# Sums in the fold on VectorE, a narrowing cut in four, and half a sum between two multiply-adds

## The chip, the core and the metric

The kernel runs on one core of a Trainium2 chip. The metric is the device time of one execution in microseconds (us), the median of several runs. Five engines work side by side, each through its own queue in order: TensorE (matmuls, PE in the profile; PEld are its weight loads), VectorE (DVE), ScalarE (ACT), GpSimd (POOL) and SyncE (SP, which here issues DMAs). They wait for each other through semaphores.

## The reference

```python
# x: (8, 3136, 256); w_in: (256, 1024); conv_w: (3, 1024); w_out: (1024, 256), all float32
X = np.fft.fft(x, axis=1)
X = np.fft.fft(X, axis=2)
x = X.real

h = np.maximum(x @ w_in, 0.0)
hp = h with one row of zeros in front of and behind each sequence
conv_out = sum(conv_w[k] * hp[:, k:k + 3136, :] for k in range(3))
gate = 1.0 / (1.0 + np.exp(-conv_out))
out = (h * gate) @ w_out
```

A two-dimensional Fourier transform whose real part is kept, then a feed-forward block whose gate is a convolution of three taps along the sequence.

## The kernel before

**The transform.** The Fourier transform along the sequence is a product with cosine and sine tables. Symmetry is used first: rows of x are added to and subtracted from each other (the "fold"), so that a quarter of the sequence is left to multiply. The rows of a batch come in two halves, each a tile `xh` of up to 99 partitions and eight row blocks of 512 values: four by a plain DMA of SyncE, four in reverse order by indirect DMAs of POOL (L132). `fold_ops(b)` returns seven pieces for each half: `pair(0)` and `pair(2)` (L157) add the mirrored blocks; `both(6, subtract)` (L168) writes the differences of blocks 0, 1 and 2, 3 into blocks 6, 7; `feats(1)` (L189, L190, and small copies on POOL, L191) folds these along the features into a tile `w`; then the sums of blocks 0, 1 and 2, 3; `evens` (L173, L174) adds and subtracts the two sums; `feats(0)` folds that.

The sums have two forms. For batch 0 they are one VectorE instruction, `both(4, add)`. For the other seven batches they are `sums` (L177), an accumulating DMA issued by POOL that adds blocks 2, 3 into blocks 0, 1 of the same tile; `evens` then reads blocks 0, 1 and writes 4, 5.

Nine "units" of matmuls for batch 0 and eight for each later one multiply `w` by the tables (tile `pd`); ScalarE copies one part out of PSUM (L290, L309) and VectorE finishes (`u.fin`: L294, L297, L313, L315, L325, L327) into the tiles `pt` and `qt`.

**The steps.** The feature transform is merged into `w_in`, giving the weights `G`. What remains runs in 256 steps (b, c, f): 8 batches, 4 chunks of the sequence, 8 blocks of 128 features. A step has `seed` (ScalarE, L657, a start value into the PSUM tile `pa`), `products` (TensorE, `pa` and `pb`), `copies` (ScalarE, L689, `pb` scaled into `nb`), `combine` (VectorE, L700, two instructions: `pa` plus `nb` gives the front half of `h`, `pa` minus `nb` the back half, both cut at zero), `first_tap` (ScalarE, L706), `tap` 1 and 2 (VectorE, L711, one multiply-add each), `sigmoid` (ScalarE, L724, in two parts), `gate` (VectorE L732 and POOL L731, one part each; L734 for a rest) and `mm2` (TensorE, `po`, the product with `w_out`; after the eighth feature block ScalarE copies to `os`, L751, and SyncE stores). In steps 3 to 19 (`triple`) TensorE does a third product and ScalarE writes the front half of `h` (L686), and `combine` has one instruction.

**The order.** Everything is recorded by one loop over cycles t, and each engine runs its share in the order of recording. Cycle t holds `sigmoid` of step t-2; `products` and `copies` of step t+1; `combine` of step t, `seed` of step t+2 and `first_tap` of step t; `tap` 1 of step t-1; side work "dve"; `tap` 2 of step t-1; `gate` of step t-2; side work "load"; `mm2` of step t-3; side work "pe". `at(cycle, where, fn)` lists the side work: fold pieces and finishes are under "dve", loads and, before the change, `sums` under "load". `ends` = [9, 20, 36, 61, 93, ...] spreads each batch's fold and units over the steps of the batches before it: batch 1 is folded in cycles 9 to 19, batch 2 in 20 to 35, batch 3 in 36 to 60. `free` keeps the fold pieces of batches 2 and up out of cycles that have a finish or a piece already. Tiles rotate: `pa` has two buffers, `nb` two, `h` four, `g` five, `os` three, `xh` two.

**The narrowing.** The weights come as 64-bit numbers, and VectorE makes 32-bit ones of them: exponent (`power`: L528, then ScalarE L530), mask of the fraction (L542), the low word added to it (L543), the sign (L536), the product (L546). `w_in[3]` and four parts of `w_out` are narrowed within the steps, in cycles 0, 2, 3, 5 and 7: `power` at the cycle's start ("first"), the four others between the two taps ("dve").

Of the kernel before, what the change touches and what calls it, by code (L numbers as in the profile page):

```python
# [11 lines left out]
U32 = mybir.dt.uint32  # L12
AF = mybir.ActivationFunctionType
ALU = mybir.AluOpType
# [19 lines left out]
BIG = 3.4028234663852886e38  # L34
# [3 lines left out]
def kernel(  # L38
# [10 lines left out]
    nc = tc.nc  # L49
# [12 lines left out]
    NF = F // P  # L62
# [24 lines left out]
    vt = nc.vector.tensor_tensor  # L87
    gt = nc.gpsimd.tensor_tensor
    stt = nc.vector.scalar_tensor_tensor
# [12 lines left out]
    xh, wt, ea = {}, {}, {}  # L102
# [39 lines left out]
    def fold_ops(b):  # L142

        def half(h):
            k = slice(0, NP if h == 0 else KR)
            qs = slice(2 * h, 2 * h + 2)

            def t():
                return xh[b, h]

            def pair(m):
                def f():
                    a, r = t()[k, m:m + 2], t()[k, 7 - m:5 - m:-1, ::-1, :]
                    vt(a[:, :, :, 1:D], a[:, :, :, 1:D], r[:, :, :, D - 1:0:-1], op=ALU.add)  # L157
                    if m == 2:
                        a, r = t()[k, 0:4], t()[k, 7:3:-1, ::-1, :]
                        vt(a[:, :, :, 0], a[:, :, :, 0], r[:, :, :, 0], op=ALU.add)  # L160
                return f

            def flat(i, j):
                return t()[k, i:j].rearrange("p s q d -> p (s q d)")

            def both(to, op):
                def f():
                    vt(flat(to, to + 2), flat(0, 2), flat(2, 4), op=op)  # L168
                return f

            def evens():
                f, to = (0, 4) if b else (4, 0)
                vt(flat(to, to + 1), flat(f, f + 1), flat(f + 1, f + 2), op=ALU.add)  # L173
                vt(flat(to + 1, to + 2), flat(f, f + 1), flat(f + 1, f + 2), op=ALU.subtract)  # L174

            def sums():
                nc.gpsimd.dma_start(out=flat(0, 2), in_=flat(2, 4), accum_op=ALU.add)  # L177

            def feats(odd):
                def f():  # L180
                    if h == 0 and odd:
                        wt[b] = [wp.tile([P, 4, HQ, P], F32, name="w", tag="w%d" % i) for i in range(2)]
                        if b == 0:
                            ea[b] = ep.tile([P, 2, HQ], F32, name="ea", tag="ea")
                            nc.gpsimd.memset(wt[b][0][0:KR, 2:4, :, P - 1:P], 0.0)
                    w, s = wt[b][odd], 6 if odd else 4 if b else 0
                    v = t()[k, s:s + 2]
                    lo, hi = v[:, :, :, 1:P], v[:, :, :, D - 1:P:-1]
                    vt(w[k, 0:2, qs, 1:P], lo, hi, op=ALU.add)  # L189
                    vt(w[k, 2:4, qs, 0:P - 1], lo, hi, op=ALU.subtract)  # L190
                    nc.gpsimd.tensor_copy(w[k, 0:2, qs, 0], v[:, :, :, 0])  # L191
                    if b:
                        nc.gpsimd.memset(wt[b][odd][k, 2:4, qs, P - 1:P], 0.0)
                    elif odd:
                        gt(w[k, 2:4, qs, P - 1], t()[k, 7:5:-1, :, P], sg[k], op=ALU.mult)
                    else:
                        nc.gpsimd.tensor_copy(ea[b][k, :, qs], v[:, :, :, P])
                return f

            return [pair(0), pair(2), both(6, ALU.subtract), feats(1), sums if b else both(4, ALU.add),  # L200
                    evens, feats(0)]

        return half(0) + half(1)


# [62 lines left out]
    def product(o, w, st, q, cols, start, stop):  # L268

        def f(p):  # L270
            k = KR if q == HQ - 1 else NP
            mm(p[o], w(k, q), table(k, st, q, cols), start, stop)
        return f
# [240 lines left out]
    def narrow(dst, raw, room=None):  # L514


        ts = nc.vector.tensor_scalar
        lsl, lsr = ALU.logical_shift_left, ALU.logical_shift_right
        lo, hi = raw[:, :, :, 0], raw[:, :, :, 1]
        lof, d = lo.bitcast(F32), dst.bitcast(I32)  # L520
        sg = hi
        if room is not None:
            c, n = hi.shape[1:]
            sg = room[:, 0:c * n].rearrange("p (c n) -> p c n", c=c)

        def power():

            ts(out=d, in0=hi, scalar1=20, scalar2=0x7FF, op0=lsr, op1=ALU.bitwise_and)  # L528
            if room is not None:
                act(d, d, AF.Relu, scale=2.0 ** 23, bias=low[0:d.shape[0]])  # L530
            else:
                ts(out=d, in0=d, scalar1=-896, scalar2=0, op0=ALU.add, op1=ALU.max)
                ts(out=d, in0=d, scalar1=23, scalar2=None, op0=lsl)

        def sign():
            stt(out=d, in0=hi, scalar=-0x80000000, in1=d, op0=ALU.bitwise_and, op1=ALU.bitwise_or)  # L536

        def product():

            if room is None:  # L540
                sign()
            ts(out=sg, in0=hi, scalar1=0xFFFFF, scalar2=0x100000, op0=ALU.bitwise_and, op1=ALU.bitwise_or)  # L542
            stt(out=lof, in0=lo.bitcast(U32), scalar=2.0 ** -32, in1=sg, op0=ALU.mult, op1=ALU.add)  # L543
            if room is not None:
                sign()
            stt(out=dst, in0=lof, scalar=2.0 ** -20, in1=dst, op0=ALU.mult, op1=ALU.mult)  # L546
        return power, product

    class Weight:

# [108 lines left out]
    def triple(s):  # L659

        return s[0] == 0 and TRIPLE[0] <= s[1] * NF + s[2] < TRIPLE[1]
# [26 lines left out]
            for i, cols in enumerate((ch.fcols, ch.cols)):  # L688
                act(nb[s][:, i, cols], p[:, cols], AF.Copy, scale=-1.0 if i else 1.0)  # L689

    def combine(s):

        ch, n, fs = cut(s)
        a, c = pa.pop(s), nb.pop(s)
        if not triple(s):
            row_of(s)
        h = hs[s]
        for i, (to, cols) in enumerate(((h[:, ch.front], ch.fcols), (h[:, ch.back][:, ::-1], ch.cols))):
            if i or not triple(s):
                nc.vector._custom_dve(TENSOR_ADD_SAT, out=to, in0=a[:, cols], in1=c[:, i, cols],  # L700
                                      s0=BIG, s1=0.0)

    def first_tap(s):
        n = chunks[s[1]].w - 2
# [3 lines left out]
    def tap(s, k):  # L708
        g, h, f = gs[s], hs[s], s[2]
        n = g.shape[1]  # L710
        stt(out=g, in0=h[:, k:k + n], scalar=cw[:, k, f:f + 1], in1=g, op0=ALU.mult, op1=ALU.add)  # L711
# [14 lines left out]
    def gate(s):  # L726

        b, c, f = s
        g, h = gs[s], hs.pop(s)[:, 1:]
        v, p, r = shares(s)  # L730
        gt(g[:, p], g[:, p], h[:, p], op=ALU.mult)  # L731
        vt(g[:, v], g[:, v], h[:, v], op=ALU.mult)  # L732
        if r.start < r.stop:
            gt(left[:, f, b % 2 * LEFT:(b % 2 + 1) * LEFT], g[:, r], h[:, r], op=ALU.mult)  # L734
# [81 lines left out]
    side = {}  # L816

    def at(cycle, where, fn):
        side.setdefault((cycle, where), []).append(fn)
# [4 lines left out]
    room = left[:, NF // 2:].rearrange("p f i -> p (f i)").bitcast(I32)  # L824

    def shared(cycle, w, c):
        for where, fn in zip(("first", "dve"), w.parts(c, c + 2, room)):
            at(cycle, where, fn)

    shared(0, w_in[3], 0)  # L830
# [43 lines left out]
        at(cs[-1] - 2, "load", lambda b=b: spread(b, range(len(chunks) - 1)))  # L874
        at(per * b + 1, "load", lambda b=b: spread(b, [len(chunks) - 1]))
    for b in range(1, B):

        ops = fold_ops(b)
        sums = [ops.pop(11), ops.pop(4)]
        m = len(ops) // 2  # L880
        c0, n = ends[b - 1], ends[b] - ends[b - 1]
        cs = [free(c0 + j * n // len(ops)) if b > 1 else c0 + j * n // len(ops) for j in range(len(ops))]
        assert cs[-1] < ends[b] and (b > 1 or cs[m] > NF + 3)
        if b + 1 < B:
            for h in range(2):
                for j, fn in enumerate(load_ops(b + 1, h, nc.sync)):
                    at(cs[m * h + m - 1] + 1 + j, "load", fn)
        for j, fn in enumerate(ops):
            at(cs[j], "dve", fn)
            if j % m == 2:  # L890
                at(cs[j], "load", sums.pop())

# [7 lines left out]
    for t in range(n + LAG):  # L902
        def run(where):
            for fn in side.get((t, where), []):
                fn()
        if 0 <= t - 2 < n:
            sigmoid(steps[t - 2])
        run("first")
        if t + 1 < n:
            products(steps[t + 1])  # L910
            copies(steps[t + 1])
        run("act")
        if t < n:
            combine(steps[t])
        if t + 2 < n:
            seed(steps[t + 2])
        if t < n:
            first_tap(steps[t])

        if 0 <= t - 1 < n:  # L920
            tap(steps[t - 1], 1)
        run("dve")
        if 0 <= t - 1 < n:
            tap(steps[t - 1], 2)
        if 0 <= t - 2 < n:
            gate(steps[t - 2])
        run("load")
        if t >= LAG:
            mm2(steps[t - LAG])
        run("pe")  # L930
# [66 lines left out]
```

## Time and profile before

| what | value |
|---|---|
| median of 3 runs | 1204.5 us (1204.35, 1204.5, 1206.42) |
| the profiled execution's own time | 1206.42 us |
| its span, first to last instruction | 1204.7 us |
| granted TensorE clock, mean | 0.999 |
| TensorE busy | 1170.8 us, 97% |
| VectorE busy | 1111.8 us, 92% |
| ScalarE busy | 883.8 us, 73% |
| GpSimd busy | 480.7 us, 40% |
| accumulating DMAs in the fold (L177) | 14, of 392 or 396 KB each, 5.3 and 5.6 us to landing |
| VectorE taps (L711) | 512, mean 1128 ns |
| VectorE half sums (L700) | 495, mean 557 ns |

In the profile's lines "DVE L173 xh<-xh" is VectorE's instruction of line 173 that writes and reads a tile `xh`. An "idle before" or a bracket with an arrow names what ended the time in which the engine stood still before the instruction. Ends of matmuls are modelled, so TensorE's busy share says less than the distance between starts.

### The profile page before, as it was taken

What the parts mean: (1) busy time and instruction counts of PE and PEld (TensorE: products, weight loads), DVE (VectorE), ACT (ScalarE), POOL (GpSimd) and SP (SyncE); (2) the same over time, 40 slices, a digit from 0 to 9 for tenths busy, and PEclk for the clock granted to TensorE, in tenths of its full rate; (3) what the DMA queues carried; (4) which work ended last, traced back from release to release, by engine and by line L of the source; (5) the groups of instructions that cost most, each with busy time, mean ns of one, the idle gap of its engine ahead of it and who ended that gap; (6) DMA issues with size and microseconds to landing.
All of it is one profiled execution on the core that took longest, in us unless ns stands there. A gap on an engine that the chain in (4) does not pass through costs nothing.

```text
span 1204.7 us, 15375 instructions
## 1 busy us (share of the span) xinstructions
PE 1170.8 (97%) x4836; PEld 901.5 (75%) x4836; DVE 1111.8 (92%) x1611; ACT 883.8 (73%) x1840; POOL 480.7 (40%) x554
## 2 busy tenths in 40 slices
PE   4999999999999999999999999999999999999998
PEld 2776677677777777777777777777778777777776
DVE  7898899999998999999997999999998988899996
ACT  2677657777776877778776877777777777788884
POOL 5225646463362333624244242542234323342224
PEclk9999999999999999999999999999999999999999
DMA  9713343222132221212122021320101000110000
GB/s 227 188 34 94 83 54 106 70 67 75 19 101 51 67 54 36 75 38 80 41 87 65 6 75 41 94 54 27 41 22 32 31 27 27 47 34 27 27 27 30
DMA packets 71859, 71.73 MB, mean 60 GB/s; under 512 B 28520, under 2 KB 58096, under 8 KB 71779
## 3 DMA queue, kind: packets, MB, share of 16 engines
q1 hardware_dynamic: 64349, 51.98, 15.3%
q0 software_dynamic: 6912, 18.50, 6.6%
q8 instruction: 38, 0.62, 0.2%
q10 hardware_dynamic: 518, 0.28, 0.1%
q14 instruction: 42, 0.34, 0.1%
HBM read 39.33 MB, written 25.74 MB: 54 GB/s over the span
## 4 chain that ended last, share of the span: by engine, by line
PE 84%; DVE 5%; POOL 3%; issue 3%; ACT 2%; DMA 2%; ACTq 0%; POOLq 0%; DVEq 0%; SPq 0%
PE po L93 51%; PE pb L93 13%; PE pa L93 13%; PE pd L93 7%; DVE g L711 2%; POOL xh L132 1%; DMA out_dram<-os 1%; POOL g L731 1%; DMA xh<-xh 1%; DVE h L700 1%; ACT nb L689 1%; DVE g L732 1%; ACT os L751 0%; POOL left L734 0%; ACT g L724 0%
## 5 line engine op out<-in xcount | busy, mean ns | idle before, releaser
L93 PE MATMUL po<-wout,g 128*128 128x256 f32 x3072 | 706.1, 379 | 8.2 <-DVE g L732 6.5
L93 PEld LDWEIGHTS po<-wout,g 128*128 128x128 f32 x3072 | 580.9, 190 | 152.4 <-issue 17.9
L711 DVE SCALAR_TENSOR_TENSOR g<-h,cw,g 128x770 f32<-128x770 f32 (+1 forms) x512 | 577.5, 1128 | 7.6 <-ACT g L706 3.4
L731 POOL TENSOR_TENSOR g<-g,h 128x385 f32<-128x385 f32 (+1 forms) x256 | 263.4, 1031 | 639.9 <-ACT g L724 422.7
L689 ACT ACTIVATE nb<-pb 128x386 f32<-128x386 f32 (+2 forms) x478 | 212.6, 499 | 167.1 <-PE pb L93 166.1
L724 ACT ACTIVATE g<-g 128x385 f32<-128x385 f32 (+2 forms) x512 | 244.5, 529 | 90.4 <-DVE g L711 89.4
L700 DVE CUSTOM_DVE_ANT_0 h<-pa,nb 128x386 f32<-128x386 f32 (+2 forms) x495 | 256.4, 557 | 4.9 <-POOL h L667 3.3
L706 ACT ACTIVATE g<-h,cw 128x770 f32<-128x770 f32 (+1 forms) x256 | 243.9, 953 | 0.0
L93 PE MATMUL pb<-qt,G 127*128 127x387 f32 (+2 forms) x512 | 212.9, 496 | 5.0 <-ACT nb L689 3.4
L93 PE MATMUL pa<-pt,G 128*128 128x387 f32 (+2 forms) x512 | 211.9, 494 | 0.0
L732 DVE TENSOR_TENSOR g<-g,h 128x385 f32<-128x385 f32 (+1 forms) x256 | 147.3, 575 | 10.4 <-ACT g L724 10.4
L657 ACT ACTIVATE pa<-eb,ge 128x387 f32<-128x387 f32 (+2 forms) x256 | 154.5, 604 | 1.7 <-DVE h L700 0.9
L93 PEld LDWEIGHTS pa<-pt,G 128*128 128x128 f32 x512 | 96.7, 189 | 73.7 <-issue 18.4
L93 PE MATMUL pd<-tab,w 98*128 98x196 f32 (+3 forms) x448 | 126.7, 374 | 0.0
L93 PEld LDWEIGHTS pb<-qt,G 127*128 127x128 f32 x512 | 93.8, 190 | 23.7 <-ACT nb L689 4.7
L132 POOL DMA_INDIRECT xh<-in_x_dram,idx x64 | 102.6, 1604 | 13.5 <-issue 9.7
L93 PEld LDWEIGHTS pd<-tab,w 98*128 98x128 f32 (+1 forms) x448 | 84.7, 191 | 12.3
L751 ACT COPY os<-po 128x256 f32<-128x256 f32 x196 | 57.5, 390 | 15.4 <-DMA out_dram<-os 10.7
L734 POOL TENSOR_TENSOR left<-g,h 128x64 f32<-128x64 f32 x64 | 64.9, 1014 | 0.0
L157 DVE TENSOR_TENSOR xh<-xh 98x1020 f32<-98x1020 f32 (+1 forms) x32 | 39.5, 1238 | 2.7 <-DMA xh<-in_x_dram,idx 2.6
L191 POOL COPY w<-xh 98x4 f32<-98x4 f32 (+1 forms) x32 | 27.1, 846 | 13.3 <-DVE xh L174 9.2
L189 DVE TENSOR_TENSOR w<-xh 98x508 f32<-98x508 f32 (+1 forms) x32 | 25.6, 799 | 0.1
(119 smaller groups left out, 378.4 us busy)
## 6 DMA issues: line engine op xcount, KB each, us to landing
out_dram<-os SPq DMA_DIRECT2D x192, 128.0 KB
xh<-in_x_dram SPq DMA_DIRECT2D x16, 784.0 KB
eb<-ed SPq DMA_DIRECT2D x16, 193.5 KB
xh<-xh POOLq DMA_DIRECT2D x7, 396.0 KB, 5.6
xh<-xh POOLq DMA_DIRECT2D x7, 392.0 KB, 5.3
tab<-dft_seq_dram SPq DMA_DIRECT2D x4, 589.5 KB
raw<-in_moe_w_in_dram SPq DMA_DIRECT2D x4, 512.0 KB
raw<-in_moe_w_out_dram SPq DMA_DIRECT2D x1, 2048.0 KB
```

What stands on the lines that cost most here:

```text
L93: nc.tensor.matmul(o, l, r, start=start, stop=stop, skip_group_check=True)
L132: nc.gpsimd.indirect_dma_start(out=xh[b, h][0:NP, 7 - m].rearrange("p q d -> p (q d)"), out_offset=None, in_=bass.AP(tensor=x.tensor, offs ...
L657: act(pa[s][:, 0:n], eb[b, c], AF.Copy, scale=ge[:, f:f + 1])
L689: act(nb[s][:, i, cols], p[:, cols], AF.Copy, scale=-1.0 if i else 1.0)
L700: nc.vector._custom_dve(TENSOR_ADD_SAT, out=to, in0=a[:, cols], in1=c[:, i, cols], s0=BIG, s1=0.0)
L706: act(gs[s], hs[s][:, 0:n], AF.Copy, scale=cw[:, 0, s[2]:s[2] + 1])
L711: stt(out=g, in0=h[:, k:k + n], scalar=cw[:, k, f:f + 1], in1=g, op0=ALU.mult, op1=ALU.add)
L724: act(gs[s][:, c], gs[s][:, c], AF.Sigmoid)
L731: gt(g[:, p], g[:, p], h[:, p], op=ALU.mult)
L732: vt(g[:, v], g[:, v], h[:, v], op=ALU.mult)
L734: gt(left[:, f, b % 2 * LEFT:(b % 2 + 1) * LEFT], g[:, r], h[:, r], op=ALU.mult)
L751: nc.scalar.copy(out=osb[:, j % 2], in_=pt[:, j % 2])
```

## The change

Three things are changed.

1. `sums` is gone. Every batch forms the sums by `both(4, add)` on VectorE into blocks 4, 5, and `evens` reads 4, 5 and writes 0, 1 (before, that was batch 0 only). The list of fold pieces has 14 entries for every batch, where VectorE's list had 12 before, and they are spread over the same cycles.
2. The part of the narrowing behind `power` is cut in three: `high` (mask and sign) stays between the taps ("dve"); `significand` runs behind the second tap ("late"); `product` runs behind the gate ("last").
3. `combine` is called for each half by itself. In cycles with no side work under "dve" the second half now runs between `tap` 1 and `tap` 2; in the others both halves run before `tap` 1, as before. `seed` and `first_tap` are recorded behind that.

VectorE has 1314 rows in its order before and 1522 behind the change (repeated instructions that follow each other are one row), POOL 442 and 422; TensorE, ScalarE and SyncE keep theirs.

```diff
             def evens():
-                f, to = (0, 4) if b else (4, 0)
-                vt(flat(to, to + 1), flat(f, f + 1), flat(f + 1, f + 2), op=ALU.add)
-                vt(flat(to + 1, to + 2), flat(f, f + 1), flat(f + 1, f + 2), op=ALU.subtract)
-
-            def sums():
-                nc.gpsimd.dma_start(out=flat(0, 2), in_=flat(2, 4), accum_op=ALU.add)
+                vt(flat(0, 1), flat(4, 5), flat(5, 6), op=ALU.add)
+                vt(flat(1, 2), flat(4, 5), flat(5, 6), op=ALU.subtract)
...
-                    w, s = wt[b][odd], 6 if odd else 4 if b else 0
+                    w, s = wt[b][odd], 6 * odd
...
-            return [pair(0), pair(2), both(6, ALU.subtract), feats(1), sums if b else both(4, ALU.add),
-                    evens, feats(0)]
+            return [pair(0), pair(2), both(6, ALU.subtract), feats(1), both(4, ALU.add), evens,
+                    feats(0)]
...
-        def product():
-
+        def high():
             if room is None:
                 sign()
             ts(out=sg, in0=hi, scalar1=0xFFFFF, scalar2=0x100000, op0=ALU.bitwise_and, op1=ALU.bitwise_or)
-            stt(out=lof, in0=lo.bitcast(U32), scalar=2.0 ** -32, in1=sg, op0=ALU.mult, op1=ALU.add)
             if room is not None:
                 sign()
+
+        def significand():
+
+            stt(out=lof, in0=lo.bitcast(U32), scalar=2.0 ** -32, in1=sg, op0=ALU.mult, op1=ALU.add)
+
+        def product():
             stt(out=dst, in0=lof, scalar=2.0 ** -20, in1=dst, op0=ALU.mult, op1=ALU.mult)
-        return power, product
+        return power, high, significand, product
...
-    def combine(s):
+    def combine(s, i):
 
         ch, n, fs = cut(s)
-        a, c = pa.pop(s), nb.pop(s)
-        if not triple(s):
+        if i == 0 and triple(s):
+            return
+        if i == 0:
             row_of(s)
-        h = hs[s]
-        for i, (to, cols) in enumerate(((h[:, ch.front], ch.fcols), (h[:, ch.back][:, ::-1], ch.cols))):
-            if i or not triple(s):
-                nc.vector._custom_dve(TENSOR_ADD_SAT, out=to, in0=a[:, cols], in1=c[:, i, cols],
-                                      s0=BIG, s1=0.0)
+        a, c, h = pa[s], nb[s], hs[s]
+        to, cols = ((h[:, ch.front], ch.fcols), (h[:, ch.back][:, ::-1], ch.cols))[i]
+        nc.vector._custom_dve(TENSOR_ADD_SAT, out=to, in0=a[:, cols], in1=c[:, i, cols], s0=BIG, s1=0.0)
...
-        for where, fn in zip(("first", "dve"), w.parts(c, c + 2, room)):
+        for where, fn in zip(("first", "dve", "late", "last"), w.parts(c, c + 2, room)):
             at(cycle, where, fn)
...
         ops = fold_ops(b)
-        sums = [ops.pop(11), ops.pop(4)]
-        m = len(ops) // 2
         c0, n = ends[b - 1], ends[b] - ends[b - 1]
...
         for j, fn in enumerate(ops):
             at(cs[j], "dve", fn)
-            if j % m == 2:
-                at(cs[j], "load", sums.pop())
...
         run("act")
+        alone = not side.get((t, "dve"))
         if t < n:
-            combine(steps[t])
+            combine(steps[t], 0)
+            if not alone:
+                combine(steps[t], 1)
+        if 0 <= t - 1 < n:
+            tap(steps[t - 1], 1)
+        if t < n and alone:
+            combine(steps[t], 1)
+        run("dve")
         if t + 2 < n:
             seed(steps[t + 2])
         if t < n:
             first_tap(steps[t])
-
-        if 0 <= t - 1 < n:
-            tap(steps[t - 1], 1)
-        run("dve")
         if 0 <= t - 1 < n:
             tap(steps[t - 1], 2)
+        run("late")
         if 0 <= t - 2 < n:
             gate(steps[t - 2])
+        run("last")
         run("load")
```

More of the change, by code (lines that the diff above doesn't have):

```diff
@@ L878 @@
         ops = fold_ops(b)
-        sums = [ops.pop(11), ops.pop(4)]
-        m = len(ops) // 2
         c0, n = ends[b - 1], ends[b] - ends[b - 1]
         cs = [free(c0 + j * n // len(ops)) if b > 1 else c0 + j * n // len(ops) for j in range(len(ops))]
-        assert cs[-1] < ends[b] and (b > 1 or cs[m] > NF + 3)
+        assert cs[-1] < ends[b] and (b > 1 or cs[7] > NF + 3)
         if b + 1 < B:
@@ L886 @@
                 for j, fn in enumerate(load_ops(b + 1, h, nc.sync)):
-                    at(cs[m * h + m - 1] + 1 + j, "load", fn)
+                    at(cs[7 * h + 6] + 1 + j, "load", fn)
         for j, fn in enumerate(ops):
             at(cs[j], "dve", fn)
-            if j % m == 2:
-                at(cs[j], "load", sums.pop())
     LAG = 3
```

## The prediction

> **What bounds the kernel now.** I read the page's busy shares first, then the chain that ended last, a table of windows, the waits, and the timelines of the few places where TensorE stands still.
>
> The page's head, the chain in a quiet stretch (start, length, what), and the stretches of the span (length, then busy time and instructions of each engine, clock, DMA):
>
> ```profile
> PE 1170.8 (97%) x4836; PEld 901.5 (75%) x4836; DVE 1111.8 (92%) x1611; ACT 883.8 (73%) x1840; POOL 480.7 (40%) x554
> ```
> ```profile
> 77.24 2.60 PE po L93 x12
> 79.84 0.65 PE pb L93 x2
> 80.50 1.31 PE pa L93 x4
> 81.80 2.59 PE po L93 x12
> ```
> ```profile
> 100.00:150.00 50.00, 44.46 (x179) 31.50 (x178) 39.91 (x56) 33.28 (x85) 30.83 (x26) 1.00 0.35 91
> 200.00:240.00 40.00, 38.20 (x158) 27.28 (x157) 38.83 (x57) 28.33 (x60) 22.47 (x28) 1.00 0.28 72
> 240.00:365.00 125.00, 125.00 (x524) 98.05 (x523) 119.01 (x178) 93.21 (x191) 62.40 (x62) 1.00 0.23 65
> 365.00:380.00 15.00, 14.22 (x57) 10.43 (x56) 11.42 (x17) 9.79 (x24) 4.16 (x6) 1.00 0.37 89
> 645.00:665.00 20.00, 17.34 (x70) 12.89 (x69) 14.21 (x21) 12.28 (x29) 4.58 (x10) 1.00 0.31 77
> 665.00:1184.00 519.00, 518.87 (x2145) 404.11 (x2144) 490.93 (x693) 405.99 (x838) 174.89 (x204) 1.00 0.12 37
> ```
>
> TensorE bounds it: 125.00 of 125 and 518.87 of 519 busy. A cycle is 12 output records at 0.216 plus four product records at 0.326, 3.90 us, or 4.55 with the third product (cycles 3 to 19), and nothing in the change touches TensorE's order. So a gain can come only from places where TensorE waits behind the start-up, and a loss only from VectorE outgrowing TensorE. I measured each cycle as the distance between first output matmuls, less its own matmuls at those rates; this counts the slow restarts that busy time hides. Lost behind 62 us: 1.1 in cycles 3 to 10, **7.8 in cycles 11 to 20** (100 to 154 us), **3.9 in cycles 29 to 37** (201 to 240), **4.0 in cycles 67 and 131** (371 and 654), 0.9 elsewhere. The waits that carry it, and the places:
>
> ```profile
> DVE xh L173 <- DMA xh<-xh: 8.0, 2, 4.6
> ACT os L751 <- DMA out_dram<-os: 10.7, 4, 5.6
> ```
> ```profile
> 103.89 1.00 DVE L711 SCALAR_TENSOR_TENSOR g<-h,cw,g 128x770 f32<-128x770 f32 x1
> 109.53 0.69 DVE L173 TENSOR_TENSOR xh<-xh 98x512 f32<-98x512 f32 x1 [4.63 <-DMA xh<-xh]
> ```
> ```profile
> 652.59 1.73 ACT L751 COPY os<-po 128x256 f32<-128x256 f32 x6
> 659.92 0.37 ACT L751 COPY os<-po 128x256 f32<-128x256 f32 x1 [5.60 <-DMA out_dram<-os]
> ```
> ```profile
> 661.94 0.92 PE L93 MATMUL pb<-qt,G 127*128 127x386 f32 x2 [2.66 <-ACT nb L689]
> ```
>
> The accumulating DMA (POOL's L177, 14 of them, 5.3 to 5.6 us to landing) is in both. In cycles 12 and 18 VectorE's L173 waits for it, 4.63 and 3.39 us, with gate and second tap behind it in the queue. At 368.8 and 651.9 it starts 1.1 us before six output stores; their landing is late, ScalarE stands 3.7 and 5.6 us before an output copy, its next nb copies come late and TensorE waits. At 937.5, with no such DMA near, the same copy waits 1.03 us and TensorE loses nothing.
>
> **The change part by part.** All times us.
>
> *The sums' DMA goes.* Off POOL: 14 issues of 1.03 and their waits for L168 (11.1). POOL's indirect loads and gates queued behind them move up. On VectorE: 14 sums like L168 (1.22 long; next instruction 1.13 after the start), 15.9, 2.26 a batch for seven batches.
>
> (A) *Batch 1, cycles 9 to 20.* Fourteen pieces now share the eleven cycles from 9: the first half's new sum shares cycle 12 with the evens, the second subtraction shares cycle 16 with its features, the second sum takes cycle 17, evens 18, features 19. VectorE's cycle, from gate to gate without waits, beside TensorE's work (cycle: VectorE / TensorE):
> 9: 5.66/4.53; 10: 4.39/4.53; 11: 4.00/4.53; 12: 4.13+1.13+0.12 = 5.38/4.53; 13: 4.51/4.53; 14: 4.44/5.10; 15: 5.35/4.53; 16: 3.93+1.19+0.12 = 5.24/5.67; 17: 4.00-1.19+1.13 = 3.94/4.53; 18: 4.39/3.88; 19: 4.51/3.88; 20: 4.43/5.20.
> The 0.12 is a dependent pair's bubble (below). VectorE enters with its gate 1.3 ahead (1.34 now at cycle 8). Carrying lead + TensorE - VectorE, never under 0.06, TensorE waits 0.07 at cycle 12, 0.14 at 15, 0.12 at 19: 0.33. VectorE sums to 55.8 against 55.5, so it is a draw, and collisions with POOL can add 0.5 in each of the five cycles that show none now (11, 12, 16, 17, 18). I take one: 0.8 in place of 7.8, **-7.0**, from -7.5 (0.3 left) to -5.0. In cycle 16 POOL's gate stands behind the feature copy (0.85), which waits for that cycle's subtraction; it ends about with VectorE's gate and is in that allowance.
>
> (B) *Narrowing, cycles 0, 2, 3, 5, 7.* Same instructions (0.42, 0.69 twice, 0.69). The sign goes second, the significand behind the second tap, the product behind the gate. Now the gate's cycle with a narrowing is 5.67, the next 3.4, together TensorE's 9.06, and the lead swings from 0.1 to 1.3. The gate comes about 0.7 earlier in those cycles, so 1.1 of loss becomes 0.7, **-0.4**. Against it: in cycle 2 the sign waits for ScalarE's L530 (done at 59.18) with only the mask ahead of it, so a wait of 1.11 becomes about 2.1; the product then ends about 62.5, and the first output matmul starts at 62.58 now. Bounds +0.6 and -1.1.
>
> (C) *Batch 2, cycles 20 to 37*, where VectorE is late. The two sums (2.26) land in cycles 24 and 33. Around 24 TensorE has 5.3 to 6.6 a cycle and VectorE idles 1.2, 1.3 and 1.0 for ScalarE's copies at cycles 23, 24 and 27, so the first is absorbed. In the second half the carry gives TensorE waits of 0.47, 0.83, 0.75, 0.81 (cycles 29 to 32), 0.3, 0.6, 0.19, 0.28 (34 to 37): 4.2 to 4.3 against 3.9. **+0.4**. Bounds: both sums on the path, +2.3; collisions in cycles 29, 31 and 33 (0.76, 0.71, 0.58) gone, -2.1.
>
> (D) *Output stores* at 371 and 654 meet no sums: **-3.9** of 4.0. Bounds 0 and -4.0.
>
> (E) *Batches 3 to 7*: 11.3 more on VectorE, over some 175 cycles in which its lead is mostly 1 to 4 us and it idles about 1 us at most of the eight table finishes of a batch. From 380 to 645 it is busy 253.6 of 265, and 4.5 joins: TensorE hides it. If that cover went, it would be 11.3. **0**, bounds +1 and -0.4.
>
> (F) *The half sum between the taps.* 106 cycles have it. Two taps in a row start 1.047 apart; a tap and an independent instruction 0.937: 0.11 for each, about 12 of VectorE's time, nearly all where TensorE bounds: **0** on the span. Moved past the tap, the half sum ends 0.93 later (1.45 if a tap collides). ScalarE's seed of two cycles on waits for that, then first tap, then sigmoid. In the last batch the seed mostly starts 1.66 after the sum's end and is done 2.35 before TensorE's product: 4.0 of room. The least among the 106 is 2.2 (cycle 96), so it is hidden. SP's order of stores and loads is as before.
>
> The Trainium skill ("VectorE: DVE Perf Modes", The DRAIN you can't avoid) says that chaining operations or adding semaphores costs nothing beyond a flush after each, which would make F and B's bubbles worth 0; the rows above give 0.11 a pair. By the page the bubbles in A fall away and none is saved in B and F: the sum would differ by 0.3 at most, since TensorE hides the rest. The same skill ("SBUF — State Buffer", SBUF: two separate sides) calls the port that VectorE and GpSimd share an exclusive lock, for operations with two SBUF inputs too: that speaks against 14 new ones. This trace agrees that collisions exist (taps of 1.51 against 1.01), and the page gives no other price.
>
> **Sum:** -7.0 - 0.4 + 0.4 - 3.9 = -10.9. The profiled execution took 1206.4 (span 1204.7), the median is 1204.5: 1193.8 in a span, **1193.6** for the median.
>
> **The rivals.**
> *The gain is half eaten.* VectorE at a draw in cycles 9 to 20 turns the DMA's wait into its own lateness. For it: 55.8 against 55.5, and 3.9 lost already in cycles 29 to 37. Against: no other wait of its size there. A keeps 4, C pays 2.3: 1198.5.
> *The change doesn't do what it says for the stores.* They wait anyway, since the copies outrun three os buffers (1.03 at 937.5). Then D is 0: 1197.5. Against: that wait cost TensorE nothing.
> *VectorE becomes the bound in batches 3 to 7* (slower). Ten sums at 1.13 on the path and a port collision of 0.5 each, 16.3: 1209.9. It decides only when VectorE's work in 265 us rises by over 11.4; the sums bring 4.5, and fourteen collisions on top would bring it level.
> *The late half sum* (slower) makes ScalarE's seeds late. Past its room of 2.2 to 4.0, say by 0.5 in each of the last 35 cycles: 1211. The delay is at most 1.45.
>
> **How the numbers follow.** Forecast 0.74, half eaten 0.09, stores 0.06; VectorE bound 0.05, late seeds 0.03; the draw that leaves nothing, 0.03. About 0.2% (2.4 us) is what a measurement here can tell from no change: faster 0.89, same 0.03, slower 0.08. The likeliest case alone: 1193.6 - 0.5 (A) - 2.5 (C) = 1190.6 up to 1193.6 + 2.0 (A) + 1.9 (C) = 1197.5. Taking in the two middle rivals and something of their sum (1202.4), the range is 1190.0 to 1201.5.
>
> **What would show it.** Right: no L177 rows; TensorE busy again about 1171 in a span of 1194; its idle time in 100 to 150 under 1; no ScalarE wait over about 1 before output copies at cycles 67 and 131; first waits of TensorE near 200 to 230 of VectorE's gate, about as now; tap pairs without the 0.11 in quiet cycles. Wrong: waits of TensorE for the gate in batches 3 to 7, for seeds (ScalarE L657), or for POOL's gate around cycle 16; output copies that wait 4 us with no DMA beside them.

## The result, and the profile after

The changed kernel takes 1200.2 us (median of 1198.98 to 1200.4) beside 1205.4 for the kernel before on the same chip: a ratio of 0.9955, 95% interval [0.9938, 0.9972]. Timed a second time, on another occasion, it took 1198.8 beside 1205.6, 0.9942 [0.9922, 0.9962]. The forecast was 1193.6: the sign is right and the time lies inside the range, but of the 10.9 us only about half came: 5.2, and 6.8 the second time. One of the rivals, "the gain is half eaten", gave 1198.5; how it came so near stands below.

The profiled execution took 1198.98, its span is 1197.2. Its busy times, its waits at the two places that the prediction named (with the wait for VectorE's gate of the kernel before ahead of them, there L732), and the stretches of the span (length, then busy time and instructions of PE, PEld, DVE, ACT, POOL, clock, DMA share, GB/s):

```profile
PE 1170.0 (98%) x4836; PEld 901.2 (75%) x4836; DVE 1124.4 (94%) x1625; ACT 884.7 (74%) x1840; POOL 502.6 (42%) x540
```
```profile
PE po L93 <- DVE g L732: 6.5, 8, 2.2
```
```profile
PE po L93 <- DVE g L731: 5.5, 12, 1.9
...
ACT os L750 <- DMA out_dram<-os: 5.3, 4, 3.0
```
```profile
100.00:150.00 50.00, 47.53 (x195) 34.55 (x194) 49.93 (x63) 34.75 (x88) 26.72 (x24) 1.00 0.30 81
200.00:240.00 40.00, 38.44 (x160) 27.62 (x159) 40.00 (x58) 27.69 (x58) 21.00 (x27) 1.00 0.19 56
240.00:365.00 125.00, 125.00 (x521) 97.60 (x520) 122.95 (x180) 93.50 (x193) 58.28 (x60) 1.00 0.18 57
365.00:380.00 15.00, 15.00 (x62) 11.44 (x61) 14.20 (x22) 11.97 (x27) 5.92 (x8) 1.00 0.20 63
645.00:665.00 20.00, 19.93 (x80) 14.83 (x79) 17.72 (x27) 14.97 (x34) 5.50 (x10) 1.00 0.15 47
665.00:1176.00 511.00, 510.82 (x2113) 398.04 (x2112) 475.00 (x684) 401.27 (x827) 190.77 (x194) 1.00 0.11 35
```

At 365 and 645 TensorE is busy again (15.00 of 15 and 19.93 of 20, against 14.22 and 17.34), and from 240 on it hardly stands. From 100 to 150 it gained little over half of what it lacked: 47.53 of 50, where it had 44.46, and there VectorE has become the engine that is always busy (49.93, where it had 39.91). VectorE's waits for the accumulating DMA are gone from the list. What is left of TensorE's waits there is for VectorE's gate alone: 2.9 us from 88 to 154, where it was 4.1 for that gate and 1.5 for GpSimd's.

For the accounting I use the prediction's measure: the distance between the first output matmuls of two cycles, less the cycle's own matmuls at the rates of the kernel before. In the two kernels without the accumulating DMA that were profiled twice it repeats within 0.02 in cycles 9 to 20 and 29 to 37; with it, it varies by more (below). Us lost, by cycles:

| kernel | 3 to 8 | 9 to 20 | 29 to 37 | 67 and 131 | elsewhere |
|---|---|---|---|---|---|
| before | 1.09 | 7.86 | 3.87 | 4.02 | 6.19 |
| after | 1.07 | 4.98 | 4.22 | 0.38 | 6.38 |
| after, second time | 1.08 | 4.96 | 4.22 | 0.20 | 6.37 |

(The column "elsewhere" is 0.02 to 0.03 a cycle, the rounding of the rates; only its change of +0.19 means anything, and 0.1 of that lies in cycle 38, at the end of batch 2's fold.) The cycles gained 6.0. The two profiled spans differ by 7.5, because in the one of after the first output matmul came at 61.08, and in the one of before at 62.58. Over all fourteen profiled executions of this study that start lies anywhere from 60.75 to 63.62, and for one and the same kernel 1.2 apart, so those 1.5 us are not credited to the change. Between the medians lie 5.2 and 6.8.

### The profile page after: what moved, and what is told of

Read it like the earlier page. It is cut to its first block, busy times and chain, and to the rows that moved or that the text cites. A ratio compares the mean times of both kernels' runs of the same rounds, so it can differ in the third digit from the quotient of the medians.

```text
span 1197.2 us, 15485 instructions
## 1 busy us (share of the span) xinstructions
PE 1170.0 (98%) x4836; PEld 901.2 (75%) x4836; DVE 1124.4 (94%) x1625; ACT 884.7 (74%) x1840; POOL 502.6 (42%) x540
## 4 chain that ended last, share of the span: by engine, by line
PE 83%; DVE 11%; issue 2%; ACT 2%; POOL 1%; DMA 1%; ACTq 0%; DVEq 0%; SPq 0%; POOLq 0%
PE po L93 50%; PE pb L93 13%; PE pa L93 12%; PE pd L93 8%; DVE g L710 5%; DVE h L700 1%; DVE g L731 1%; POOL xh L132 1%; DVE xh L157 1%; ACT nb L689 1%; DMA out_dram<-os 0%; DVE xh L168 0%; DVE raw L543 0%; DVE w L186 0%; ACT os L750 0%
## 5 line engine op out<-in xcount | busy, mean ns | idle before, releaser
L710 DVE SCALAR_TENSOR_TENSOR g<-h,cw,g 128x770 f32<-128x770 f32 (+1 forms) x512 | 585.3, 1143 | 17.4 <-ACT g L705 17.1
L730 POOL TENSOR_TENSOR g<-g,h 128x385 f32<-128x385 f32 (+1 forms) x256 | 284.5, 1112 | 607.2 <-ACT g L723 395.1
L700 DVE CUSTOM_DVE_ANT_0 h<-pa,nb 128x386 f32<-128x386 f32 (+2 forms) x495 | 264.1, 555 | 1.6 <-POOL h L667 1.6
L731 DVE TENSOR_TENSOR g<-g,h 128x385 f32<-128x385 f32 (+1 forms) x256 | 145.1, 567 | 3.7 <-ACT g L723 3.5
L733 POOL TENSOR_TENSOR left<-g,h 128x64 f32<-128x64 f32 x64 | 67.6, 1057 | 0.0
L187 POOL COPY w<-xh 98x4 f32<-98x4 f32 (+1 forms) x32 | 34.9, 1090 | 39.0 <-DVE xh L168 26.4
L168 DVE TENSOR_TENSOR xh<-xh 98x1024 f32<-98x1024 f32 (+1 forms) x32 | 38.9, 1216 | 0.1
```

## Where batch 1 lost what it should have gained

The largest loss left is in cycle 12 (2.09). VectorE there, then GpSimd, then TensorE, all of the kernel after (start, length, instruction, in brackets the idle time before it and what ended it):

```profile
102.67 0.55 DVE L700 CUSTOM_DVE_ANT_0 h<-pa,nb 128x386 f32<-128x386 f32 x1
103.14 3.17 DVE L710 SCALAR_TENSOR_TENSOR g<-h,cw,g 128x770 f32<-128x770 f32 x1
106.24 1.21 DVE L168 TENSOR_TENSOR xh<-xh 98x1024 f32<-98x1024 f32 x1
```
```profile
99.90 3.69 POOL L132 DMA_INDIRECT xh<-in_x_dram,idx  x1 [0.30 <-ACT nb L684]
103.60 0.20 POOL L187 COPY w<-xh 98x4 f32<-98x4 f32 x1
103.73 0.12 POOL L189 MEMSET w<- 98x4 f32 x1
103.80 1.69 POOL L730 TENSOR_TENSOR g<-g,h 128x385 f32<-128x385 f32 x2
```
```profile
110.23 1.13 PE L93 MATMUL po<-wout,g 128*128 128x256 f32 x4 [1.90 <-DVE g L731]
```

A tap that takes 1.01 alone takes 3.17. GpSimd has been in three indirect loads for 8 us, from 95.59, so its own work has piled up behind them; when the last load ends at 103.59, it runs a copy, a memset and two gates without a gap until 105.49, and the tap ends 0.82 later. Cycle 17 has the same in small: an indirect load up to 131.49, one gate up to 132.40, and the tap that started at 130.98 takes 2.25. In the kernel before the same backlog is there (POOL, kernel before):

```profile
100.65 3.69 POOL L132 DMA_INDIRECT xh<-in_x_dram,idx  x1 [0.30 <-ACT nb L684]
104.34 1.09 POOL L177 DMA_DIRECT2D xh<-xh  x1
...
105.22 2.10 POOL L731 TENSOR_TENSOR g<-g,h 128x385 f32<-128x385 f32 x2
```

But there VectorE's tap was over at 104.89 and VectorE stood until 109.53 for the accumulating DMA. GpSimd's gates ran in that wait and met nothing. The wait that the change removes had been hiding collisions that no row of the trace before could show.

## The experiments

The theory after the result: in cycles 9 to 20 VectorE is held by GpSimd's instructions on the port that the two share, and that ate the gain. Rivals: the 14 new sums are simply too much work for VectorE; the narrowing or the half sum between the taps brought the loss; the accumulating DMA was not what held the output stores. Ratios are to the kernel before on the same chip.

### Which part of the change does what

The sums alone (the fold's hunks of the change and nothing else):

```diff
...
-            def sums():
-                nc.gpsimd.dma_start(out=flat(0, 2), in_=flat(2, 4), accum_op=ALU.add)
...
-            return [pair(0), pair(2), both(6, ALU.subtract), feats(1), sums if b else both(4, ALU.add),
-                    evens, feats(0)]
+            return [pair(0), pair(2), both(6, ALU.subtract), feats(1), both(4, ALU.add), evens,
+                    feats(0)]
...
```

> The kernel before with the first part of the change alone (all sums on VectorE, 14 fold pieces). Theory (the sums carry the gain, and VectorE collides with POOL's late gates in batch 1): TensorE loses about 4.5 to 5.5 us in cycles 9 to 20 where the kernel before loses 7.8, nothing in cycle 67 and at most 0.4 in cycle 131 (4.0 before): about 5 to 6 us faster than before, as the whole change is. Rival (the other two parts carry a good share): 3 us or less faster.

Measured: 1198.4, ratio 0.9935 [0.9918, 0.9951]. Losses: 4.22 in cycles 9 to 20, a little under what was expected, 4.22 in 29 to 37, 0.12 in 67 and 131.

Everything but the sums (the kernel after with these hunks taken back):

```diff
...
-            return [pair(0), pair(2), both(6, ALU.subtract), feats(1), both(4, ALU.add), evens,
-                    feats(0)]
+            return [pair(0), pair(2), both(6, ALU.subtract), feats(1), sums if b else both(4, ALU.add),
+                    evens, feats(0)]
...
```

> The changed kernel with its sums put back on the accumulating DMA; the narrowing in four and the half sum between the taps stay. Theory: both are hidden by TensorE, so the time is that of the kernel before within 1 us, with the losses in cycles 11 to 20, 67 and 131 back. Rival: 2 us or more faster than before (they help) or slower (the narrowing's new order costs in cycles 3 to 10).

Measured: 1205.2, ratio 0.9998 [0.9985, 1.0011]; 7.36 lost in cycles 9 to 20, 3.87 in 29 to 37, 3.96 in 67 and 131. The stretches of the two kernels around the output stores, sums alone first:

```profile
365.00:380.00 15.00, 15.00 (x62) 11.43 (x61) 14.16 (x23) 11.96 (x28) 4.75 (x9) 1.00 0.20 63
645.00:665.00 20.00, 20.00 (x82) 15.16 (x81) 18.41 (x26) 15.65 (x35) 5.48 (x10) 1.00 0.15 47
```
```profile
365.00:380.00 15.00, 14.19 (x57) 10.39 (x56) 10.88 (x15) 10.50 (x25) 3.38 (x6) 1.00 0.37 89
645.00:665.00 20.00, 17.42 (x71) 13.04 (x70) 14.11 (x22) 12.81 (x29) 4.27 (x8) 1.00 0.29 67
```

The whole gain comes from the sums; on the time of the kernel, narrowing and half sum together are worth nothing that can be measured. By the cycles they cost 0.76 where the sums are on VectorE: cycles 9 to 20 lose 4.98 with them and 4.22 without, most of it in cycle 9 (below). TensorE loses its time at the stores where the DMA is and not where it isn't.

Batch 1 alone back on the DMA, from the kernel after:

```diff
+    def DMA_SUMS(b):
+        return b == 1
...
-            return [pair(0), pair(2), both(6, ALU.subtract), feats(1), both(4, ALU.add), evens,
+            return [pair(0), pair(2), both(6, ALU.subtract), feats(1), sums if dma else both(4, ALU.add), evens,
                     feats(0)]
...
+        sums = [ops.pop(11), ops.pop(4)] if DMA_SUMS(b) else []
...
```

> The changed kernel with batch 1 alone put back on the accumulating DMA with its 12 pieces; batches 2 to 7 form the sums on VectorE. Theory: in cycles 9 to 20 the loss goes from 5.6 back to about 7.8 and the rest stays, so 2 to 3 us slower than the changed kernel. Rival (VectorE's sums in batch 1 cost as much as the DMA's wait): the same time as the changed kernel.

Measured: 1203.1, ratio 0.9966 [0.9948, 0.9985]; 8.40 lost in cycles 9 to 20, 4.20 in 29 to 37, 0.16 in 67 and 131. So batch 1 is worth 3.4 by the cycles, the stores 3.9.

The two other parts, each alone, from the kernel before. Narrowing in four places:

```diff
-        def product():
-
+        def high():
...
+        def significand():
...
-        return power, product
+        return power, high, significand, product
...
-        for where, fn in zip(("first", "dve"), w.parts(c, c + 2, room)):
+        for where, fn in zip(("first", "dve", "late", "last"), w.parts(c, c + 2, room)):
```

> The kernel before with the second part alone (narrowing in four places; sums on the DMA, both half sums ahead of the first tap). If the narrowing's new places bring what was seen in cycles 3 to 8 (loss 0.55 in place of 1.09 with parts two and three together) and the half sum causes the new 0.60 in cycle 9: 0.5 to 0.6 in cycles 3 to 8, and 0.1 or less in cycle 9. If the narrowing causes cycle 9's loss too, 0.6 there.

Measured, one execution: 1203.9 beside 1206.0; cycles 3 to 8 lose 0.51 in place of 1.09, nearly all of the difference in cycle 3 (0.30 in place of 0.80), cycles 9 to 20 lose 7.46.

The half sum between the taps:

```diff
...
+        alone = not side.get((t, "dve"))
         if t < n:
-            combine(steps[t])
+            combine(steps[t], 0)
+            if not alone:
+                combine(steps[t], 1)
+        if 0 <= t - 1 < n:
+            tap(steps[t - 1], 1)
+        if t < n and alone:
+            combine(steps[t], 1)
...
```

> The kernel before with the third part alone (second half sum between the taps in cycles without side work). If the half sum causes cycle 9's loss: 0.6 there and about 1.1 in cycles 3 to 8. Either way the loss behind cycle 37, apart from cycles 67 and 131, stays within 0.3 of the kernel before's (38 to 66: 0.74; 68 to 130: 1.96; 132 to 257: 3.19), since TensorE hides VectorE's saving of 0.11 a pair.

> The half of the sums between the two multiply-adds alone, timed in rounds. If the single look (4 us above before) was right in the main: cycles 9 to 20 lose 9.3 us and cycle 131 4.0 us again, 2.5 us more than before in all, and the ratio is 1.001 to 1.003. If the prediction's price of nothing for this part holds: ratio 0.999 to 1.001 and cycle losses as before, 7.9 and 2.95.

Measured first in one execution: 1210.1 beside 1206.0, with 9.34 lost in cycles 9 to 20 and 4.04 in cycle 131. Timed in rounds: 1206.7, ratio 1.0007 [0.9995, 1.0018], with 7.77 and 3.00, and 1.68 more than before in cycle 132. Most of what had looked like a price of 4 us lies in cycles where the accumulating DMA or the stores are waited for, which this kernel still has, and it differs between the two executions: cycles 18 and 19 lost 4.09 together in the first and 2.61 in the second, before 2.38. In cycle 132, beside the stores, they lost 0.50 and 1.68 more than before, so that the first expectation, within 0.3 there, failed. What both executions show alike is 0.39 in cycle 7.

One effect belongs to neither part alone. Cycle 9 loses 0.03 before, 0.02 with the narrowing, 0.03 with the half sum, and 0.60 with both (after, and the kernel without the sums). There VectorE's first pair of batch 1 is held behind a gate of GpSimd (VectorE, then GpSimd, kernel after; the pair's two instructions take 2.34 before, and 2.34 again where GpSimd has no gates there, in the gate edit below):

```profile
89.86 3.01 DVE L157 TENSOR_TENSOR xh<-xh 98x1020 f32<-98x1020 f32 x2
```
```profile
89.23 1.44 POOL L730 TENSOR_TENSOR g<-g,h 128x385 f32<-128x385 f32 x1 [3.37 <-issue]
```

The half sum moves VectorE by one tap against GpSimd, and the narrowing leaves it less lead to pay with: the gate's lead at that point is 0.74 after, 1.76 with the half sum alone, where the pair takes 3.01 too and costs TensorE nothing.

### Is it the port?

All of the gate on VectorE in the cycles of batch 1's fold, so that GpSimd has no gates there, only its loads, copies and memsets; VectorE takes over 0.4 us a cycle:

```diff
+        if b == 0 and 5 <= c * NF + f < 19:
+            vt(g[:, v.start:p.stop], g[:, v.start:p.stop], h[:, v.start:p.stop], op=ALU.mult)
+            return
         gt(g[:, p], g[:, p], h[:, p], op=ALU.mult)
         vt(g[:, v], g[:, v], h[:, v], op=ALU.mult)
```

> The changed kernel with POOL's part of the gate done by VectorE in cycles 7 to 20 (one gate of 770 columns, 0.46 longer a cycle); POOL keeps its indirect loads and the feature copies there. Theory (POOL's gates hold the port that VectorE needs): no tap in cycles 9 to 20 takes over 1.1 us, cycle 12 of VectorE falls from 7.42 to about 5.8, VectorE's twelve cycles from 60.6 to about 58, and TensorE's loss in cycles 9 to 20 from 5.0 to 3.5 or less. Rival (the indirect loads hold it by themselves): the taps of 3.17 in cycle 12 and 2.25 in cycle 17 stay over 1.5.

> The gate edit alone, timed in rounds. Port theory: cycles 9 to 20 lose 1.9 us again against 4.98 after, and the time is 2.5 to 3.5 us below that of the kernel after on the same chip, ratio to before about 0.991. Rival (the gain in the single look was its start-up): no more than 1 us below the kernel after.

Measured: 1195.6 in one execution, and 1195.7 in rounds, ratio 0.9913 [0.9891, 0.9934]; the kernel after took 1198.8 on that chip. Cycles 9 to 20 lose 1.92 and 1.93 in place of 4.98. VectorE at the place of the long tap, TensorE's waits for the gate (L731 in the edited cycles 7 to 20, L734 in all others), and the stretch from 100 to 150 (the last line from the execution in rounds):

```profile
102.43 0.54 DVE L700 CUSTOM_DVE_ANT_0 h<-pa,nb 128x386 f32<-128x386 f32 x1
102.90 1.00 DVE L710 SCALAR_TENSOR_TENSOR g<-h,cw,g 128x770 f32<-128x770 f32 x1
103.83 1.21 DVE L168 TENSOR_TENSOR xh<-xh 98x1024 f32<-98x1024 f32 x1
```
```profile
PE po L93 <- DVE g L734: 2.7, 8, 0.5
PE po L93 <- DVE g L731: 0.5, 1, 0.5
```
```profile
100.00:150.00 50.00, 49.53 (x206) 37.07 (x205) 49.93 (x69) 37.31 (x89) 20.11 (x11) 1.00 0.29 69
```

VectorE has more to do and is less late: its twelve cycles take 57.5 in place of 60.65, with 4.8 more work in them. With GpSimd's gates away every tap from 78 to 147 us takes between 1.00 and 1.02, so the gates are the cause of 3.06 of the 4.98. The loads moved with this edit, and none runs beside the tap in cycle 12; but three taps of 1.01 (130.24, 132.52, 134.65) run beside loads from 128.96 to 137.37, which answers the rival.

The Trainium skill ("SBUF — State Buffer", SBUF: two separate sides) calls the shared port an exclusive lock that the instruction that starts first keeps for its whole length. These runs agree that one engine's instruction is held while the other's run, and that the port is what they share is taken from the page, not from a run. They differ in one thing: by the recorded starts the tap of 3.17 was first, 103.14 against 103.60, and yet it was the one held. One tap paid for 1.9 us of GpSimd's instructions that stood in line.

The indirect loads thinned to one a cycle from cycle 9, so that less piles up behind them:

```diff
-        at(NF + 1 + j // 3, "load", fn)
+        at(NF + 1 + max(j - 2, 0), "load", fn)
```

> The changed kernel with the four indirect loads of batch 1's second half on POOL in cycles 9, 10, 11 and 12 in place of one in 9 and three in 10. Theory (the tap of 3.17 us in cycle 12 is held up by two POOL gates that run back to back behind a load of 3.69 us): that tap falls to at most 1.6, TensorE's loss in cycle 12 from 2.1 to under 0.8, and the kernel is about 1.5 us faster than the changed one. Rival (VectorE is too full in cycle 12 by itself): the loss in cycle 12 stays within 0.4 of 2.1.

Measured: 1197.2, ratio 0.9927 [0.991, 0.9945]; cycles 9 to 20 lose 3.99, and cycle 12 1.11 in place of 2.09, where under 0.8 was expected; 0.5 of what the kernel gained is cycle 3, which changes between executions (below). The tap in cycle 12, and GpSimd beside it:

```profile
103.27 1.52 DVE L710 SCALAR_TENSOR_TENSOR g<-h,cw,g 128x770 f32<-128x770 f32 x1
```
```profile
103.11 0.86 POOL L730 TENSOR_TENSOR g<-g,h 128x385 f32<-128x385 f32 x1 [1.33 <-issue]
104.16 1.51 POOL L132 DMA_INDIRECT xh<-in_x_dram,idx  x1 [0.19 <-issue]
```

The same gate comes alone and costs the tap 0.51, not 2.16. The size that the prediction took for a collision was right for one gate; the backlog made it four times that.

The thinned loads, no half sum between the taps, and later ends for the folds of batches 2 and 3:

```diff
-        alone = not side.get((t, "dve"))
+        alone = False
...
-    ends = [9, 20, per + 4] + [per * (b - 1) - 3 for b in range(3, B)]
+    ends = [9, 20, per + 7, 2 * per - 1] + [per * (b - 1) - 3 for b in range(4, B)]
```

> A version meant to beat both: sums on VectorE and the narrowing in four as in the changed kernel, both half sums ahead of the first tap, batch 1's indirect loads one a cycle in cycles 9 to 12, and batch 2's fold spread to cycle 38 and batch 3's to 62 in place of 35 and 60. Loss expected: cycle 9 at most 0.1, cycle 12 about 1.1, cycles 29 to 39 about 2.5 in place of 4.3: 2 us faster than the version with the loads spread, 7 to 9 us faster than the kernel before.

Measured: 1196.4, ratio 0.992 [0.9897, 0.9942]. The later ends brought nothing: cycles 29 to 37 lose 4.35, where about 2.5 was expected, and the kernel is 0.8 us below the one with thinned loads (on another chip), not 2. What it gained lies in batch 1: 2.42 in cycles 9 to 20, with cycle 9 back at 0.02 and cycle 12 at 0.23. So with the loads thinned the order of the half sum decides the rest of cycle 12, with all of GpSimd's gates in place. Why batch 2 stays late with its pieces further apart wasn't pursued.

Gate edit, thinned loads and no half sum together:

> The kernel after with three edits: all of the gate on VectorE in cycles 7 to 20, the indirect loads thinned to one a cycle from cycle 9, and the taps in the order of before (no half sum between them). Theory that GpSimd's holds of the shared port cost the remainder in batch 1: cycles 9 to 20 lose 0.8 to 1.2 us (0.36, 0.34 and 0.13 in cycles 14, 16 and 20, which every kernel shows and no wait explains, and little else), and the time is 0.9 to 1.2 us below that with the gate edit alone, a ratio to before of 0.989 to 0.991. Rival, that VectorE's own work is what is late (it takes over some 0.4 us a cycle): cycles 9 to 20 lose 1.9 or more, cycle 12 0.7 as with the gate edit alone, and the ratio is 0.991 to 0.992 or above.

Measured: 1195.5, ratio 0.9917 [0.99, 0.9934]; 1.68 lost in cycles 9 to 20, 0.65 of it in cycle 12. Here the expectation failed: it is no faster than the gate edit alone, and cycle 12 has not moved. Every instruction of VectorE in that cycle has its undisturbed length, and still it takes 5.65 from gate to gate beside TensorE's 4.53: the 0.65 is VectorE's own work, as the rival had it (sum, evens and a longer gate in one cycle). The 0.4 by which the gate is longer is the edit's own; without it, above, cycle 12 lost 0.23. Both causes exist, then; GpSimd's gates are the larger.

The kernel after once more, on that chip:

> The kernel after once more, beside the others on one chip. Expected: ratio to before 0.995, cycles 9 to 20 lose 4.98 us and cycles 29 to 37 4.2 us again, since these have come out the same in each execution; the first output matmul may come anywhere from 60.7 to 63.6 us, and the span follows it.

Measured: 1198.8, ratio 0.9942 [0.9922, 0.9962], with 4.96 and 4.22 lost in the two stretches and the first output matmul at 61.79.

The fastest kernels found are the three at 1195.5 to 1196.4, 2 to 3 us below the changed one: in batch 1 the change without GpSimd's gates, with or without the other two edits, or with its loads spread and both half sums ahead of the first tap.

## Why the prediction was right and wrong

| term | forecast | measured, by cycles |
|---|---|---|
| A, batch 1, cycles 9 to 20 | -7.0 | -2.9 |
| B, narrowing, cycles 3 to 8 | -0.4 | 0.0 |
| C, batch 2, cycles 29 to 37 | +0.4 | +0.35 |
| D, output stores, cycles 67 and 131 | -3.9 | -3.6 |
| E and F | 0 | +0.2 |
| sum | -10.9 | -6.0 |

**A is the step that failed**, in the sentence that allows 0.5 for a collision in each of five cycles and ends "I take one: 0.8 in place of 7.8". What is left is 4.98, 4.2 more than that. Three things make up the 4.98. First, 3.06 are GpSimd's gates (the gate edit takes just that away). VectorE's twelve cycles took 60.65; the prediction's entries add up to 56.2 (not to the 55.8 that it gives for them), so collisions beyond those that the entries already held cost VectorE 4.4, nearly all of it in three instructions: 2.16 in cycle 12, 1.24 in 17, 0.88 in 16. They fall in cycles that the prediction had named, but it priced them by the taps that collide in the trace before, at 1.51 against 1.01, and that trace had no collision behind a backlog, since VectorE was waiting there. Secondly, 0.70 of both the 7.86 and the 4.98 was never a wait for VectorE: cycles 14 and 16 lose 0.36 and 0.34 in all fourteen executions, with or without the DMA. They hold the small matmuls `pd<-ft`, and the starts around these lie up to 0.43 apart, which the nominal rates left out. (The 0.13 that cycle 13 loses in all but one is the restart behind cycle 12's wait: its first two output matmuls start 0.32 apart, the others 0.216.) The rest, 1.2, is of the kind that the prediction did count: VectorE's own work, above all in cycle 12, and a lead at the entry that was taken as 1.3 and found to be 0.74.

**B** came in part of the executions. Cycle 3 lost 0.79 to 0.81 in each of the four without the narrowing; with it, 0.3 in some and 0.8 in others, the kernel after among the latter both times, and once each way for the gate edit alone. What decides it was not found. The 0.57 that cycle 9 lost by narrowing and half sum together was not foreseen, and is counted under A.

**C** was right in size: VectorE is late there, the first sum is absorbed (cycles 21 to 28 take what they took before), and the second costs a fraction of its length.

**D** was right in its effect. Around 651 us ScalarE still waits for a store before an output copy, and TensorE hardly notices (ScalarE, kernel after):

```profile
647.64 1.74 ACT L750 COPY os<-po 128x256 f32<-128x256 f32 x6
652.38 0.37 ACT L750 COPY os<-po 128x256 f32<-128x256 f32 x1 [3.00 <-DMA out_dram<-os]
```

The wait is 3.0 in place of 5.6, and the lead over TensorE covers that: cycles 67 and 131 lose 0.38 together. The sign that I had set, no wait over about 1 before these copies, failed here; at 368 it held (0.98, before 3.7). The rival "they wait anyway" was right about the copies, and wrong about the time.

**E** held: from 240 on TensorE has no wait worth naming, with VectorE at 122.95 of 125 where it was at 119.01. **F** held: the half sum alone is at 1.0007. The seeds do wait for it, as the delay of 0.93 to 1.45 said they would, and from 240 on it stays hidden (kernel after; the same wait has 0.9 in all before):

```profile
ACT pa L657 <- DVE h L700: 25.2, 31, 1.8
```

In batch 1 the price of nothing was too low: 0.39 in cycle 7 with the half sum alone, 0.57 in cycle 9 with the narrowing.

The rival "half eaten" had A right in kind (VectorE's lateness takes the place of the DMA's wait, 2.9 of 7.0 kept) and C wrong (2.3 against 0.35). That its 1198.5 lies so near the measured time is luck: it had 1.1 too much gain in A and about 2 too much loss in C. The two slower rivals didn't come: behind 240 us TensorE's matmuls wait 0.3 for the gate in all, and never for the seeds. The profile's sign that I had set for A, under 1 us of idle time of TensorE from 100 to 150, read 2.5.

## What to carry to other kernels

Where an engine stands in a long wait, the trace can show its other instructions at their undisturbed length. Before a removed wait is counted as gain, lay what the other user of the shared port does in that time beside the instructions that will move into it, backlog and all: here one held instruction cost the sum of what stood in line (2.16 for 1.89), not one collision (0.51). When two engines come out level, the lead at the entry and each collision decide the time, so give such a term the pessimistic end of its bounds.

## What was not expected of the hardware

- A VectorE multiply-add of 1.01 us took 3.17 behind a copy, a memset and two gates of GpSimd (1.89 us in line) that followed an indirect load of 3.69; behind one gate after such a load it took 2.25, behind one gate alone 1.52. The tap's recorded start lies 0.46 and 0.51 before the end of the load in the first two. In the kernel before a tap of 1.00 ran beside the same load from 103.89 to 104.89, so the load by itself doesn't hold it. Why the tap that started first gave way to gates that started later stays open.
- Moving a gate's half from GpSimd to VectorE, the busier engine, made VectorE less late: 1.92 lost in place of 4.98.
- An accumulating DMA of the fold, gone from the queue, shortened ScalarE's wait for an output store from 5.6 to 3.0 us in cycle 131 and from 3.7 to 1.0 in cycle 67. What the rest is made of no run here shows.
- The start before the first output matmul varied from 60.75 to 63.62 us between executions, more than several of the effects sought here.
